# Attention with a bias table and a feed-forward layer: batch 1's v staged in fp32 and cast by GpSimd, q and k transposed by head, the band table loaded pair by pair

## The chip, the cores and the metric

The kernel runs on one core of one Trainium2 chip. The core has TensorE (PE: matrix products and transposes into PSUM), VectorE (DVE), ScalarE (ACT), GpSimd (POOL) and SyncE (SP, which here only issues transfers). Each engine works through its own queue in order and waits on semaphores. Transfers are issued by SP (hardware queue), by ACT (one) and by GpSimd (software queue, which alone converts types on the way); all run on the same 16 DMA engines. The metric is the device time of one execution in microseconds, the median of several runs.

## The reference

```python
B, H, S, D = 8, 8, 576, 64            # q, k, v: fp32, 0.1 * randn
scores = (q @ k.transpose(0, 1, 3, 2)) / sqrt(D)
scores = scores + bias_table[bucket].transpose(2, 0, 1)[None]   # bucket from |i - j|: 32 buckets, constant from 128 on
attn = softmax(scores)
x = (attn @ v).transpose(0, 2, 1, 3).reshape(B * S, H * D)      # 4608 x 512
h = x @ w_in                                                     # 512 x 2048
out = maximum(0.01 * h, h) @ w_out                               # 2048 x 512, fp32
```

## The kernel before, in words

**Attention.** The work is cut into 32 items: 8 batches by 4 pairs of heads. For an item n, `rows` (L385) copies q and k of the pair next to each other, `turn_by_pe` (L395) transposes them on TensorE (later items by DMA, `turn_by_dma`), `take_turned` (L407) copies the result from PSUM to `qt` and `kt`, and `apart` (L411) puts the last 64 positions of both heads apart. `score` (L432 to L440) makes the transposed scores in six units, `expo` (L446 to L453) takes their exponential on ACT, and `band` (L465) multiplies the part near the diagonal by the exponential of the bias difference (far from it the bias is constant and falls out of the softmax). `av` and `av_tail` (L485 to L503) multiply by v, which carries a column of ones for the sum; `norm` (L512, L513) divides. The result is transposed into `xT` (L527 and L531, or by DMA).

**Feed-forward.** The 4608 tokens are cut into nine tiles of 512. `ffn_in` (L544) makes 16 groups of four matmuls per tile, `ffn_act` (L549) applies the leaky relu, `ffn_out` (L556) makes the output, `ffn_y` (L561) copies it and `ffn_store` sends it.

**Buffers.** q, k and v of a batch sit in one of two sets in bf16 (`qn`, `kn`, `vn` with the first 512 positions, `v4` with the last 64). Probabilities have three sets in the first batch (`at_` twice and `spare`, in the tile `extra`), then two. The pool `gt` has two buffers, which hold `first` (raw q, k of pair 0 and raw v of batch 0) and `extra`, and later the activations of the token tiles in turn. PSUM: two tiles for scores, one for AV, three for all else.

**Loads.** Batch 0's v comes as fp32 by SP (`load_v_raw`, L312, L314) and is cast by GpSimd (`cast_v`, L333, L336). All other q, k, v and both weights come by GpSimd's queue with the cast in the transfer (`load_qk` L195, `load_v` L225 and L230, `load_v_part` L203 and L209, `load_w_in` L351, `load_w_out` L357). The table: `shift_table`, `exp_table`, `spread_table`, `copy_u_row` and `store_u_row` write one row per head to DRAM (L308); `load_hk` (L318) and `load_hk4` (L325) read it back as a band, shifted by one per partition.

**Order.** Nothing is ordered by hand past the first few lines. Each piece of work is a task in `Plan` with an engine, a cost in us, the tasks it comes after and a rank. `Plan.order` simulates the five queues with these costs and the PSUM slots, and always takes the task that can start first; the program is issued in this order, and each engine's queue keeps it. GpSimd's transfers are modelled as one ring, by `moves`; what the program's semaphores make GpSimd wait for ahead of an issue is not in the model. `run` adds matmuls on junk data (`spin`) where the plan sees TensorE idle early on. First-layer groups of a token tile have ranks from 10000, so they fill the time that attention leaves.

Of the kernel before, what the change touches and what calls it, by code (L numbers as in the profile page):

```python
# [36 lines left out]
class Plan:  # L37


    LAG = 0.25  # L40

    def __init__(self, slots):
        self.tasks = []
        self.slots = {k: [0.0] * v for k, v in slots.items()}

# [7 lines left out]
    def link(self, ins):  # L53

        for t in self.tasks:
            t["after"] = [ins[d[1:]] if isinstance(d, tuple) else d for d in t["after"]]
            t["behind"] = [d for d in t["after"] if d["engine"] == t["engine"] == "POOL"]
            t["after"] = [d for d in t["after"] if not any(d is o for o in t["behind"])]

    def order(self):  # L60
# [4 lines left out]
        first = False  # L65
        while any(waiting.values()):
# [35 lines left out]
            if t["rank"] >= 10000 and e == "PE" and not first:  # L102
                first = True
                self.slots["M"].append(r)
                t["first"] = True
# [3 lines left out]
    def run(self, fill):  # L109

        fills = True
        for t in self.order():
            if t.get("first"):
                fills = False
            if fills and t["engine"] == "PE" and t["start"] > 6.0:
# [7 lines left out]
def kernel(  # L123
# [90 lines left out]
    def load_v(b, h0, h1, by_head):  # L214
        i = b % NBUF
        p0, p1 = h0 // 2, h1 // 2
        if by_head:
            for h in range(h0, h1):
                nc.gpsimd.dma_start(
                    out=vn[i][:, :, h, 0:D],  # L220
                    in_=v[b, h, 0 : NJ * P, :].rearrange("(c s) d -> s c d", s=P),
                )
        else:
            for c in range(NJ):
                nc.gpsimd.dma_start(  # L225
                    out=vn[i][:, c, h0:h1, 0:D],
                    in_=v[b, h0:h1, c * P : (c + 1) * P, :].rearrange("h s d -> s h d"),
                )
        for e in range(2):
            nc.gpsimd.dma_start(  # L230
                out=v4[i][e * SL : (e + 1) * SL, p0:p1, e, 0:D],
                in_=v[b, h0 + e : h1 : 2, NJ * P : S, :].rearrange("h s d -> s h d"),
            )
# [18 lines left out]
    vraw_sb = first[:, qk_e : qk_e + NJ * H * D].rearrange("p (c h d) -> p c h d", c=NJ, h=H)  # L252
    vraw4 = first[:, qk_e + NJ * H * D : qk_e + (NJ * H + n_pairs) * D].rearrange("p (h d) -> p h d", h=n_pairs)
    extra = gt_pool.tile([P, n_fc, TT], BF16, name="extra", tag="gt").rearrange("p f t -> p (f t)")
    spare = extra[:, 0 : ATW + SL], extra[:, ATW + SL : ATW + SL + S + SL]
# [5 lines left out]
    load_qk(0, 2, 4)  # L261
    load_qk(0, 4, 6)
# [22 lines left out]
    clear_v(nc.gpsimd, 0)  # L285
    for i in range(3):
        clear_edges(nc.gpsimd, i)
    clear_v(nc.gpsimd, 1)
# [21 lines left out]
    def load_v_raw():  # L310
        for c in range(NJ):
            nc.sync.dma_start(out=vraw_sb[:, c, :, :], in_=v[0, :, c * P : (c + 1) * P, :].rearrange("h s d -> s h d"))  # L312
        for e in range(2):
            nc.sync.dma_start(out=vraw4[e * SL : (e + 1) * SL, :, :],  # L314
                                in_=v[0, e::2, NJ * P : S, :].rearrange("h s d -> s h d"))

# [13 lines left out]
    def cast_v(c):  # L330

        if c < NJ:
            nc.gpsimd.tensor_copy(out=vn[0][:, c, :, 0:D], in_=vraw_sb[:, c, :, :])  # L333
            return
        for e in range(2):
            nc.gpsimd.tensor_copy(out=v4[0][e * SL : (e + 1) * SL, :, e, 0:D], in_=vraw4[e * SL : (e + 1) * SL, :, :])  # L336

    def gate(t, row=0):
        nc.gpsimd.tensor_copy(out=w_in_sb[row : row + 1, 0, 0:1], in_=t)

# [11 lines left out]

    def load_w_out(half):
        if half > 1:
            return
        n = n_fc // 2
        nc.gpsimd.dma_start(  # L357
            out=w_out_sb[:, half * n : (half + 1) * n, :],
            in_=moe_w_out[half * n * P : (half + 1) * n * P, :].rearrange("(f p) e -> p f e", p=P),
        )  # L360

# [29 lines left out]

    def turn_by_pe(n, j):
        ps = turned[n, j] = ps_m_pool.tile([P, 8 * P], BF16, name="ps_t", tag="m")
        for c in range(NC):
            nc.tensor.transpose(ps[:, c * RQ : (c + 1) * RQ], in_=prs[n][0:RQ, j, c, :],  # L395
                                identity=ident[0:RQ, 0:RQ])
# [139 lines left out]
    def ffn_in(T, f0):  # L536
        t0, w = tiles[T]
        if f0 == 0:
            gts[T] = gt_pool.tile([P, n_fc, TT], BF16, name="gt", tag="gt")
        pm = pms[T, f0] = ps_m_pool.tile([P, TT], FP32, name="pm1", tag="m")  # L540
        for j in range(TT // w):
            f = f0 + j
            for c in range(n_cc):
                nc.tensor.matmul(pm[:, j * w : (j + 1) * w], lhsT=w_in_sb[:, c, f * P : (f + 1) * P],  # L544
                                 rhs=xT[c][:, t0 : t0 + w], start=(c == 0), stop=(c == n_cc - 1))

    def ffn_act(T, f0):
        t0, w = tiles[T]
        nc.scalar.activation(gts[T][:, f0 : f0 + TT // w, 0:w], pms.pop((T, f0)).rearrange("p (j t) -> p j t", t=w),  # L549
                             AF.Prelu, bias=0.0, scale=1.0, alpha=0.01)  # L550
# [17 lines left out]
    plan = Plan({"S": 2, "O": 1, "M": 2})  # L568
# [7 lines left out]
    L["raw", 0], L["raw", 1], tabl = dma(4.0), dma(4.2), dma(3.8)  # L576
    sh = add("DVE", 0.1, [tabl], shift_table, -1)
    e8t = add("ACT", 0.25, [sh], exp_table, -1)
    spr = add("PE", 0.4, [e8t], spread_table, -1, take=["O"])
    cpu = add("DVE", 0.6, [spr], copy_u_row, -1, give=["O"])  # L580
    urt = add("SP", 0.1, [cpu], store_u_row, -1, tail=2.8)
    hkt = add("SP", 0.1, [urt], lambda: load_hk(0, 2), -1, tail=3.2)
    hkr = add("SP", 0.1, [urt], lambda: (load_hk(2, H), load_hk4()), 1, tail=5.5)
    vrt = add("SP", 0.5, [urt], load_v_raw, 2, tail=6.0)
    vrt["land"] = 18.0
    L["hk", 0], L["hk", 1] = hkt, hkr
# [10 lines left out]
    QK, VB, WH = 3.9, 9.5, 5.6  # L597
    L["qk", 0, 0], L["qk", 0, 1] = dma(7.0), dma(9.5)
    pool_load(("qk", 0, 2), 1.6, lambda: (gate(ub[0:1, 0:1]), load_qk(0, 6, H)), QK / 2, after=[cpu])
    pool_load(("w_in", 0), 1.0, lambda: (gate(vraw4[SL : SL + 1, 0, 0:1], SL), load_w_in(0)), WH, after=[vrt])  # L600
    vc = [add("POOL", 0.6, [vrt] + prev, lambda c=c: cast_v(c), 0) for c in range(NJ + 1)]
    vt[0] = vc[-1]
    pool_load(("qk", 1, 0), 1.6, lambda: load_qk(1, 0, 4), QK)
    vt[1] = pool_load(("v", 1), 5.5, lambda: load_v(1, 0, H, False), VB)
    pool_load(("w_in", 1), 0.8, lambda: load_w_in(1), WH)
    pool_load(("qk", 1, 1), 1.6, lambda: load_qk(1, 4, H), QK)
    pool_load(("w_out", 0), 0.9, lambda: load_w_out(0), WH)
    pool_load(("w_out", 1), 0.9, lambda: load_w_out(1), WH)

    def plan_rows(n):  # L610
# [6 lines left out]
        if n == 0:  # L617
            r0 = add("DVE", 0.6, [L["raw", 0]], lambda: rows(0, 0), feed)
            r1 = add("ACT", 0.75, [L["raw", 1]], lambda: rows(0, 1), feed)
        else:  # L620
# [7 lines left out]
        else:  # L628
            g = [add("PE", 0.28, [(r0, r1)[j]] + sct.get(n - NQT, []) + wait, lambda j=j: turn_by_pe(n, j), feed, take=["M"])
                 for j in range(2)]  # L630
            rowt[n] = [r0, r1] + g
            src, give = g, ["M"]
        on_act = n < n_pairs - 1 or n == n_pairs
        cq = add("ACT" if on_act else "DVE", 0.6 if on_act else 0.75, [src[0]] + sct.get(n - NQT, []),
                 lambda c=nc.scalar.copy if on_act else nc.vector.tensor_copy: take_turned(n, 0, c), feed, give=give)
        on_act = n == n_pairs
        ck = add("ACT" if on_act else "DVE", 0.6 if on_act else 0.75, [src[1]] + sct.get(n - NQT, []),
                 lambda: take_turned(n, 1, nc.scalar.copy if n == n_pairs else nc.vector.tensor_copy), feed, give=give)
        on, cost = ("POOL", 0.5) if n in (1, 2) else ("DVE", 0.2)
        ak = add(on, cost, [ck], lambda: apart(n, kts[n]), feed + 1)  # L640
        aq = add(on, cost, [cq], lambda: apart(n, qts[n]), feed + 1)
# [7 lines left out]
    def plan_pair(n):  # L649
# [27 lines left out]
        sct[n] = ss  # L677
        cost = [0.43, 0.56, 0.56, 0.48, 0.25]
        bt = [add("DVE", cost[c], [es[u] for u in ([c], [c], [c], [3, 4], [5])[c]] + [L["hk", 0 if n == 0 else 1]],
                  lambda c=c: band(n, c), soon + 3) for c in range(NJ + 1)]  # L680
        done = list(es.values()) + bt + [vt[b]]
        tail_of[n] = [es[NJ + 1], bt[NJ], vt[b]]
# [25 lines left out]
    def plan_ffn(T):  # L708
# [3 lines left out]
        for f in range(n_fc):  # L712
            i = ins[T, f] = add("PE", 0.866, need + [L["w_in", int(f >= n_fc // 2)]] + (oin[T - 2] if T > 1 else []),
                                lambda f=f: ffn_in(T, f), 10000 + T * 64 + f * 4, take=["M"])
# [13 lines left out]
    for n in range(N):  # L728
        if n >= 2 * n_pairs and n % n_pairs == 0:
# [45 lines left out]
```

## Time and profile before

| | |
|---|---|
| time, median of 3 runs | 389.34 us (388.59 to 389.54) |
| time of the profiled execution | 389.1 us |
| its span, first to last instruction | 387.3 us |
| busy, us: PE, DVE, ACT, POOL | 372.1, 202.9, 241.7, 68.6 |
| mean granted TensorE clock | 0.986 |
| moved by DMA | 40.62 MB, mean 105 GB/s |

Times in the rows are in us from the start of the span, durations of one instruction in ns where marked. In rows of the order of time stand start, duration, engine, line, operation and operands, then in brackets how long the engine was idle before it and what released it. In rows of the stretches stand, for each engine, the busy time and the number of instructions, then the granted clock, the busy share of the DMA engines and what they moved. PE is a matmul, PEld a weight load. The releaser is inferred; where several semaphores were waited for, it can be the wrong one.

### The profile page before, as it was taken

What the parts mean: (1) busy time and instruction counts of PE and PEld (TensorE: products, weight loads), DVE (VectorE), ACT (ScalarE), POOL (GpSimd) and SP (SyncE); (2) the same over time, 40 slices, a digit from 0 to 9 for tenths busy, and PEclk for the clock granted to TensorE, in tenths of its full rate; (3) what the DMA queues carried; (4) which work ended last, traced back from release to release, by engine and by line L of the source; (5) the groups of instructions that cost most, each with busy time, mean ns of one, the idle gap of its engine ahead of it and who ended that gap; (6) DMA issues with size and microseconds to landing.
All of it is one profiled execution on the core that took longest, in us unless ns stands there. A gap on an engine that the chain in (4) does not pass through costs nothing.

```text
span 387.3 us, 8302 instructions
## 1 busy us (share of the span) xinstructions
PE 372.1 (96%) x3388; PEld 188.8 (49%) x3388; DVE 202.9 (52%) x539; ACT 241.7 (62%) x345; POOL 68.6 (18%) x112
## 2 busy tenths in 40 slices
PE   6859899999999999999999999999999999999995
PEld 2337455555554455555545454545545644444442
DVE  6837637878676756757565756545634411001021
ACT  4946697558975798579758875877587533333300
POOL 7168314017003300510060004000000000000000
PEclk9968999999999999999999999999999999999999
DMA  7969999759996994998399949611121100101012
GB/s 130 229 111 180 207 206 166 141 99 141 180 125 114 167 150 71 105 191 111 70 119 163 115 91 111 72 46 44 47 46 46 47 27 27 56 27 54 29 54 81
DMA packets 102741, 40.62 MB, mean 105 GB/s; under 512 B 81704, under 2 KB 97072, under 8 KB 102704
## 3 DMA queue, kind: packets, MB, share of 16 engines
q0 software_dynamic: 48512, 17.47, 42.0%
q1 hardware_dynamic: 53984, 22.33, 30.7%
q8 instruction: 26, 0.43, 0.5%
q10 hardware_dynamic: 208, 0.29, 0.3%
q14 instruction: 11, 0.09, 0.1%
HBM read 37.69 MB, written 9.45 MB: 122 GB/s over the span
## 4 chain that ended last, share of the span: by engine, by line
PE 88%; DVE 3%; SPq 3%; DMA 2%; ACT 1%; POOL 1%; issue 0%; DVEq 0%; POOLq 0%
PE pm L544 32%; PE pm L556 32%; PE ps_s L432 8%; PE ps_om L500 5%; PE ps_o L500 5%; PE ps_s L436 2%; PE ps_s L439 2%; SPq L312 1%; DMA tab<-in_bias_table_dram 1%; DVE opair L513 1%; DMA first<-in_v_dram 1%; PE ps_o L485 1%; ACT at L446 1%; DVE at L465 1%; POOL vn L333 1%; PE ps_t L395 0%
## 5 line engine op out<-in xcount | busy, mean ns | idle before, releaser
L544 PE MATMUL pm<-xT,w_in_sb 128*128 128x512 bf16 x576 | 140.6, 380 | 1.1 <-ACT gt L549 1.0
L446 ACT ACTIVATE at<-ps_s 128x1024 bf16<-128x1024 f32 x124 | 120.6, 1030 | 33.1 <-PE ps_s L432 32.5
L556 PE MATMUL pm<-w_out_sb,gt 128*128 128x512 bf16 x576 | 138.8, 380 | 0.0
L549 ACT ACTIVATE gt<-pm 128x512 bf16<-128x512 f32 x144 | 84.4, 606 | 62.1 <-PE pm L544 61.1
L465 DVE TENSOR_TENSOR at<-at,hk 128x768 bf16<-128x768 bf16 (+3 forms) x155 | 67.9, 453 | 35.3 <-ACT at L446 27.3
L556 PEld LDWEIGHTS <-gt 128*128 128x128 bf16 x576 | 53.9, 98 | 65.8 <-issue 4.7
L544 PEld LDWEIGHTS <-w_in_sb 128*128 128x128 bf16 x576 | 52.4, 98 | 65.7 <-issue 8.9
L561 DVE COPY y<-pm 128x512 f32<-128x512 f32 x36 | 24.8, 689 | 72.0 <-PE pm L556 72.0
L203 POOL DMA_DIRECT2D vn<-in_v_dram x24 | 21.6, 908 | 147.3 <-PE ps_o L500 141.6
L500 PEld LDWEIGHTS <-at 128*128 128x128 bf16 x1240 | 42.8, 99 | 6.8 <-issue 4.9
L432 PE MATMUL ps_s<-qt,kt 64*128 64x512 bf16 x256 | 40.2, 384 | 1.1 <-ACT at L453 0.3
L500 PE MATMUL ps_o<-vn,at 128*128 128x65 bf16 x640 | 27.0, 196 | 4.1 <-POOL vn L333 4.1
L448 ACT ACTIVATE at<-ps_s 128x512 bf16<-128x512 f32 x31 | 18.5, 598 | 16.7 <-PE ps_s L436 16.7
L512 DVE RECIPROCAL rcp<-ps_om 128x5 f32<-128x5 f32 x31 | 6.0, 195 | 38.6 <-PE ps_om L500 37.6
L500 PE MATMUL ps_om<-vn,at 128*128 128x65 bf16 x600 | 24.6, 196 | 0.0
L407 DVE COPY qt<-tu 128x576 bf16<-128x576 bf16 x22 | 15.6, 710 | 13.1 <-PE ps_s L440 13.1
L432 PEld LDWEIGHTS <-kt 64*128 64x128 bf16 x256 | 8.4, 94 | 27.4 <-issue 25.4
L453 ACT ACTIVATE at<-ps_s 128x576 bf16<-128x576 f32 x31 | 20.2, 652 | 0.0
L513 DVE TENSOR_TENSOR opair<-ps_o,rcp 128x320 bf16<-128x320 f32 x33 | 16.2, 492 | 1.1
L513 DVE TENSOR_TENSOR opair<-ps_om,rcp 128x320 bf16<-128x320 f32 x31 | 15.2, 492 | 1.3 <-DVE rcp L512 0.3
L407 DVE COPY kt<-tu 128x576 bf16<-128x576 bf16 x22 | 15.1, 686 | 0.0
L439 PE MATMUL ps_s<-qt,kt 128*128 128x512 bf16 x32 | 12.4, 387 | 0.9 <-ACT at L446 0.9
(80 smaller groups left out, 234.1 us busy)
## 6 DMA issues: line engine op xcount, KB each, us to landing
out_dram<-y SPq DMA_DIRECT2D x36, 256.0 KB, 2.0
qn<-in_q_dram POOLq DMA_DIRECT2D x14, 288.0 KB, 10.0
kn<-in_k_dram POOLq DMA_DIRECT2D x14, 288.0 KB, 11.7
vn<-in_v_dram POOLq DMA_DIRECT2D x28, 128.0 KB, 6.0
w_in_sb<-in_moe_w_in_dram POOLq DMA_DIRECT2D x2, 1024.0 KB, 9.7
w_out_sb<-in_moe_w_out_dram POOLq DMA_DIRECT2D x2, 1024.0 KB, 17.9
first<-in_v_dram SPq DMA_DIRECT2D x4, 256.0 KB, 6.5
hk<-u_row SPq DMA_DIRECT2D x1, 576.0 KB, 6.2
```

What stands on the lines that cost most here:

```text
L203: nc.gpsimd.dma_start(out=vn[i][:, c, :, 0:D], in_=v[b, :, c * P : (c + 1) * P, :].rearrange("h s d -> s h d"),)
L407: copy(out=t[:, 0:S].rearrange("p (r c) -> p r c", c=NC), in_=src)
L432: nc.tensor.matmul(ps[:, e, :], lhsT=kt[r, u * P : (u + 1) * P], rhs=qt[r, 0:512], start=True, stop=True)
L446: nc.scalar.activation(at[:, :, u, 0:512], ps, AF.Exp, scale=scale)
L453: nc.scalar.activation(at4[:, 0:S], ps.rearrange("p e i -> p (e i)")[:, 0:S], AF.Exp, scale=scale)
L465: nc.vector.tensor_tensor(out=o, in0=o, in1=m, op=ALU.mult)
L500: nc.tensor.matmul(ps[:, ic, :], lhsT=at[:, o : o + P], rhs=vn[i][:, c, 2 * p + e, :], start=whole and c == 0, stop=not whole and ic == NJ ...
L513: nc.vector.tensor_tensor(out=opairs[n][:, :, e * D : (e + 1) * D], in0=ps[:, :, 0:D], in1=rcp.to_broadcast([P, NJ + 1, D]), op=ALU.mult)
L544: nc.tensor.matmul(pm[:, j * w : (j + 1) * w], lhsT=w_in_sb[:, c, f * P : (f + 1) * P], rhs=xT[c][:, t0 : t0 + w], start=(c == 0), stop=(c ...
L549: nc.scalar.activation(gts[T][:, f0 : f0 + TT // w, 0:w], pms.pop((T, f0)).rearrange("p (j t) -> p j t", t=w), AF.Prelu, bias=0.0, scale=1 ...
L556: nc.tensor.matmul(ys[T, ts], lhsT=gts[T][:, f, ts * P : (ts + 1) * P], rhs=w_out_sb[:, f, :], start=(f == 0), stop=(f == n_fc - 1))
L561: nc.vector.tensor_copy(out=y, in_=ys[T, ts])
```

## The change

Batch 0's v is loaded by GpSimd's queue, not SP's, still in fp32 into `first`: heads 0 and 1 first, the other six behind (`stage_v`); `cast_v` casts them in two steps. Batch 1's v, which came with the cast in the transfer, is now staged in fp32 too, in a new tile `staged` of the pool `gt`, and cast by GpSimd. In the plan its cast has rank 35, while both halves of w_out have rank 21; its load, the second part of batch 1's q and k, and w_out are planned after pair 2's AV. Pairs 1 to 4 are transposed by head, straight from `qn` and `kn`, with 24 transposes for 12 and without `rows`. The band table is loaded with one transfer per pair. Batch 0's buffers are cleared ahead of the first loads, the others later. The one-row copies by which loads were held back (`gate`) are gone. The first two first-layer groups are split, three chunks ahead and the fourth behind. The plan has three PSUM slots for all else from its time 26 on (before: from the first first-layer group on), and some costs and ranks differ.

In GpSimd's queue as built, batch 1's cast stands behind the loads of batch 2's q, k and v:

```
... staged<-v x6 | memsets | qn,kn (batch 1, heads 4 to 7) | w_out x2 | qn,kn,qn,kn (batch 2) | vn x4, v4 x2 (batch 2) | cast vn (batch 1), v4 x2 | qn,kn (batch 3) ...
```

```diff
-    def load_v(b, h0, h1, by_head):
...
+    def stage_v(b, h0, h1):
+        m, t = stage_views(b)
+        if h1 - h0 < NJ:
             for h in range(h0, h1):
+                nc.gpsimd.dma_start(out=m[:, :, h, :], in_=v[b, h, 0 : NJ * P, :].rearrange("(c s) d -> s c d", s=P))
         else:
             for c in range(NJ):
+                nc.gpsimd.dma_start(out=m[:, c, h0:h1, :],
+                                    in_=v[b, h0:h1, c * P : (c + 1) * P, :].rearrange("h s d -> s h d"))
         for e in range(2):
+            nc.gpsimd.dma_start(out=t[e * SL : (e + 1) * SL, h0 // 2 : h1 // 2, :],
+                                in_=v[b, h0 + e : h1 : 2, NJ * P : S, :].rearrange("h s d -> s h d"))
+
+    def cast_v(b, h0, h1):
+        m, t = stage_views(b)
+        nc.gpsimd.tensor_copy(out=vn[b][:, :, h0:h1, 0:D], in_=m[:, :, h0:h1, :])
+        for e in range(2):
+            r = slice(e * SL, (e + 1) * SL)
+            nc.gpsimd.tensor_copy(out=v4[b][r, h0 // 2 : h1 // 2, e, 0:D], in_=t[r, h0 // 2 : h1 // 2, :])
...
+    def by_heads(n):
+        return 0 < n <= n_pairs
+
     def turn_by_pe(n, j):
...
+                b, p = items[n]
+                for e in range(2):
+                    nc.tensor.transpose(ps[e * D : (e + 1) * D, c * RQ : (c + 1) * RQ],
+                                        in_=(qn, kn)[j][b % NBUF][0:RQ, 2 * p + e, c, :], identity=ident[0:RQ, 0:RQ])
...
-    hkr = add("SP", 0.1, [urt], lambda: (load_hk(2, H), load_hk4()), 1, tail=5.5)
-    vrt = add("SP", 0.5, [urt], load_v_raw, 2, tail=6.0)
...
+    hk4t = add("SP", 0.1, [urt], load_hk4, 0, tail=5.0)
+    for p in range(n_pairs):
+        L["hk", p] = hkt if p == 0 else add("SP", 0.1, [urt], lambda p=p: load_hk(2 * p, 2 * p + 2), p, tail=4.2 + 2.0 * p)
...
-    pool_load(("qk", 0, 2), 1.6, lambda: (gate(ub[0:1, 0:1]), load_qk(0, 6, H)), QK / 2, after=[cpu])
-    pool_load(("w_in", 0), 1.0, lambda: (gate(vraw4[SL : SL + 1, 0, 0:1], SL), load_w_in(0)), WH, after=[vrt])
-    vc = [add("POOL", 0.6, [vrt] + prev, lambda c=c: cast_v(c), 0) for c in range(NJ + 1)]
-    vt[0] = vc[-1]
-    pool_load(("qk", 1, 0), 1.6, lambda: load_qk(1, 0, 4), QK)
-    vt[1] = pool_load(("v", 1), 5.5, lambda: load_v(1, 0, H, False), VB)
-    pool_load(("w_in", 1), 0.8, lambda: load_w_in(1), WH)
-    pool_load(("qk", 1, 1), 1.6, lambda: load_qk(1, 4, H), QK)
-    pool_load(("w_out", 0), 0.9, lambda: load_w_out(0), WH)
-    pool_load(("w_out", 1), 0.9, lambda: load_w_out(1), WH)
+    pool_load(("qk", 0, 0), 1.4, lambda: load_qk(0, 2, 4), QK / 2, after=[dma(2.4)], rank=-9)
+    pool_load(("qk", 0, 1), 1.4, lambda: load_qk(0, 4, 6), QK / 2, rank=-9)
+    pool_load(("v", 0, 0), 2.8, lambda: stage_v(0, 0, 2), VS / 4 + 1.0, rank=-9)
+    edges = add("POOL", 1.0, list(prev), lambda: [clear_edges(nc.gpsimd, i) for i in range(3)], -8)
+    pool_load(("qk", 0, 2), 1.4, lambda: load_qk(0, 6, H), QK / 2 + 1.0, rank=-8)
+    pool_load(("v", 0, 1), 4.5, lambda: stage_v(0, 2, H), 3 * VS / 4 + 1.0, rank=-5)
+    pool_load(("qk", 1, 0), 1.4, lambda: load_qk(1, 0, 4), QK, rank=-4)
+    pool_load(("w_in", 0), 0.8, lambda: load_w_in(0), WH, after=[hkr], rank=-4)
+    vt[0] = [add("POOL", 1.2, [L["v", 0, 0]], lambda: cast_v(0, 0, 2), 5),
+             add("POOL", 2.4, [L["v", 0, 1]], lambda: cast_v(0, 2, H), 5)]
+    add("POOL", 1.2, list(prev), lambda: clear_v(nc.gpsimd, 1), 9)
+    pool_load(("w_in", 1), 0.8, lambda: load_w_in(1), WH, rank=6)
+
+    def late_loads():
+        pool_load(("v", 1, 0), 5.0, lambda: (new_stage(), stage_v(1, 0, H)), VS, after=avt[2], rank=20)
+        pool_load(("qk", 1, 1), 1.4, lambda: load_qk(1, 4, H), QK, rank=20)
+        pool_load(("w_out", 0), 0.9, lambda: load_w_out(0), WO, rank=21)
+        pool_load(("w_out", 1), 0.9, lambda: load_w_out(1), WO, rank=21)
+        vt[1] = add("POOL", 3.2, [L["v", 1, 0]], lambda: cast_v(1, 0, H), 35)
...
+                early = [add("PE", 0.65, [t for p in range(n_cc - 1) for t in nmt[p]] + w + xt[n_cc - 1][:f],
+                             lambda f=f: ffn_in(T, f, range(n_cc - 1)), rank - 3, take=["M"])]
```

More of the change, by code (lines that the diff above doesn't have):

```diff
@@ L56, in link @@
             t["after"] = [ins[d[1:]] if isinstance(d, tuple) else d for d in t["after"]]
-            t["behind"] = [d for d in t["after"] if d["engine"] == t["engine"] == "POOL"]
+            t["behind"] = [d for d in t["after"] if d["engine"] == "POOL" and "moves" in t]
             t["after"] = [d for d in t["after"] if not any(d is o for o in t["behind"])]
@@ L109, in run @@
     def run(self, fill):
[L111 removed]
         for t in self.order():
[L113 to L115 removed]
+            if t["engine"] == "PE" and 6.0 < t["start"] < self.WARM:
                 k = int((t["idle"] - 0.3) / 0.25)
@@ L534, with ffn_in, ffn_act @@
     tiles = [(T * TT, TT) for T in range(n_tt)]
-    def ffn_in(T, f0):
+    def ffn_in(T, f, cs=range(n_cc)):
         t0, w = tiles[T]
[L538 to L550, printed above, removed]
+        if cs[0] == 0:
+            if f == 0:
+                gts[T] = gt_pool.tile([P, n_fc, TT], BF16, name="gt", tag="gt")
+            pms[T, f] = ps_m_pool.tile([P, TT], FP32, name="pm1", tag="m")
+        for c in cs:
+            nc.tensor.matmul(pms[T, f], lhsT=w_in_sb[:, c, f * P : (f + 1) * P], rhs=xT[c][:, t0 : t0 + w],
+                             start=(c == 0), stop=(c == n_cc - 1))
+    def ffn_act(T, f):
+        nc.scalar.activation(gts[T][:, f, :], pms.pop((T, f)), AF.Prelu, bias=0.0, scale=1.0, alpha=0.01)
     def ffn_out(T, ts, i):
```

125 lines of the change are left out of this document (51 added, 74 removed).

## The prediction

> **What bounds the kernel now.** I read the page first, then busy time by stretches, then the waits, then GpSimd's and TensorE's instructions in order of time. From the page:
>
> ```profile
> span 387.3 us, 8302 instructions
> ```
>
> The stretches (time, then busy us and instruction count of PE, PEld, DVE, ACT, POOL, then granted TensorE clock, DMA share, GB/s):
>
> ```profile
> 5.00:10.00 5.00, 3.29 (x34) 1.68 (x34) 3.50 (x9) 2.89 (x5) 3.29 (x15) 1.00 0.85 114
> 15.00:20.00 5.00, 3.84 (x21) 1.47 (x19) 4.12 (x12) 5.00 (x7) 0.00 (x0) 1.00 1.28 214
> 20.80:24.00 3.20, 0.10 (x3) 0.10 (x2) 0.67 (x2) 1.48 (x2) 1.66 (x4) 0.63 0.01 3
> 24.00:26.00 2.00, 0.85 (x5) 0.41 (x4) 0.00 (x0) 0.00 (x0) 1.95 (x4) 0.50 0.92 115
> 26.00:31.80 5.80, 5.80 (x81) 4.67 (x80) 2.91 (x8) 1.76 (x3) 5.79 (x9) 0.50 1.17 205
> 56.10:60.00 3.90, 3.78 (x80) 3.04 (x77) 2.75 (x7) 3.00 (x5) 1.51 (x2) 1.00 1.32 205
> 60.00:380.00 320.00, 319.95 (x2854) 160.22 (x2852) 165.39 (x430) 201.04 (x289) 38.57 (x51) 1.00 0.67 92
> ```
>
> From 60 us on TensorE has no gap (319.95 of 320.00), so only two things can change the end: when TensorE reaches that full stretch with how much work left, and any new hole in it. The visible hole is at 20.8 to 26, where TensorE, ACT and DMA all stand, with a half clock until 31.8. The waits say why:
>
> ```profile
> ACT extra L446 <- PE ps_s L432: 5.6, 1, 5.6
> ...
> POOL vn L203 <- DMA w_out_sb<-in_moe_w_out_dram: 4.1, 1, 4.1
> PE ps_o L500 <- POOL vn L333: 4.1, 4, 3.1
> ...
> ACT extra L453 <- PE ps_s L440: 1.3, 1, 1.3
> ```
>
> TensorE's first attention-times-v (AV) waits for GpSimd's cast of batch 0's v (L333), and ACT then waits for scores queued behind it: 5.6 + 1.3 = 6.9 us that can be had back. The other row matters more to me: GpSimd is held by a transfer. Its issue of vn waits until w_out has landed. GpSimd's queue:
>
> ```profile
> 4.13 0.57 POOL L236 MEMSET v<- 128x520 bf16 x1
> 4.75 0.26 POOL L238 MEMSET v<- 64x4 bf16 x2
> 5.07 0.24 POOL L239 MEMSET vn<- 128x32 bf16 x1
> ...
> 23.34 2.28 POOL L333 CAST vn<-first 128x512 bf16<-128x512 f32 x4
> 25.55 0.86 POOL L336 CAST v<-first 64x256 bf16<-64x256 f32 x2
> ...
> 52.22 0.87 POOL L203 DMA_DIRECT2D vn<-in_v_dram  x1 [4.14 <-DMA w_out_sb<-in_moe_w_out_dram]
> 57.86 0.88 POOL L203 DMA_DIRECT2D vn<-in_v_dram  x1 [4.76 <-PE ps_o L500]
> 58.82 0.63 POOL L209 DMA_DIRECT2D v<-in_v_dram  x1
> 60.27 0.62 POOL L209 DMA_DIRECT2D v<-in_v_dram  x1 [0.82 <-PE ps_tx L527]
> ```
>
> In the program as built, GpSimd's transfers take eight completion semaphores in turn, and each issue first waits until the transfer eight places earlier has landed. The waits of 4.14 and 4.76 us, the steps to 52.22 and from there to 57.86, are the two halves of w_out landing (the second row names a TensorE matmul, but the program has it wait for the second half of w_out and for pair 3's AV, long done). These issues load batch 2's v; nothing needs it soon, so before the change the hold is free.
>
> **The new wait.** In the changed kernel's GpSimd queue the order is: staged load of batch 1's v, rest of batch 1's q and k, both halves of w_out, batch 2's four q/k loads, batch 2's six v loads, and only then the cast of batch 1's v from its staging buffer. The fifth and sixth of batch 2's v loads wait for batch 2's first q and k loads, which sit behind both halves of w_out in the transfer queue. So the cast cannot start until everything that ends at 60.27 + 0.62 = 60.9 us before the change has been moved. TensorE's queue puts pair 4's AV, which needs that cast, behind 13 first-layer groups and ahead of all that follows; nothing passes it. Before the change that AV starts at 56.10:
>
> ```profile
> 41.09 1.03 PE L544 MATMUL pm<-xT,w_in_sb 128*128 128x512 bf16 x4
> ...
> 46.67 2.76 PE L544 MATMUL pm<-xT,w_in_sb 128*128 128x512 bf16 x12
> ...
> 56.10 0.19 PE L485 MATMUL ps_o<-v,at 64*128 64x65 bf16 x1
> ...
> 57.59 0.67 PE L395 MATMUL ps_t<-ident,pr 96*128 96x96 bf16 x12
> 58.10 1.03 PE L544 MATMUL pm<-xT,w_in_sb 128*128 128x512 bf16 x4
> ```
>
> **The sum, at that AV.** First, how much earlier the transfers run. The hole is filled, since batch 1's q and k and w_in are now issued before v's cast and not behind it: 3.2 x (1 - 3/205) + 2.0 x (1 - 115/205) = 3.15 + 0.88 = 4.0 us earlier. A second hole, 5 to 10 us, is 5 x (1 - 114/205) = 2.2 us wide; filling it could give that, but the clearing of batch 0's v buffers now stands ahead of the first issue (0.57 + 0.26 + 0.24 = 1.1 us), and small issues then follow each other at their own pace. I bound it by -1.1 and +1.1 net. Batch 1's v now arrives as fp32, twice the bytes; sizes of one load, and GpSimd's issues that waited for the first vn and the first v4 load of batch 1 before:
>
> ```profile
> vn<-in_v_dram POOLq DMA_DIRECT2D x28, 128.0 KB, 6.0
> ...
> first<-in_v_dram SPq DMA_DIRECT2D x4, 256.0 KB, 6.5
> ...
> 34.70 0.67 POOL L195 DMA_DIRECT2D kn<-in_k_dram  x1 [0.30 <-DMA vn<-in_v_dram]
> ...
> 39.39 0.67 POOL L195 DMA_DIRECT2D kn<-in_k_dram  x1 [0.58 <-DMA v<-in_v_dram]
> ```
>
> Between those two lie three loads of 128 KB and one of 32 KB, 416 KB in 4.7 us; all of it (576 KB) is then 6.5 us. Staged, 1152 KB (1.18 MB) at 205 GB/s is 5.8 us. So the rate is no worse for it; I take no difference, bounds -0.7 and +0.7. Together: 4.0 us earlier, bounds 2.2 and 5.8. Then the cast: 2.28 + 0.86 = 3.1 us by batch 0's rows (same tiles). Pair 4's AV starts at 60.9 - 4.0 + 3.1 = 60.0, bounds 58.2 and 61.8: **3.9 us later** than 56.1.
>
> Work moved ahead of it: TensorE has then done one more group of four (2.76 us for three groups, so 0.9) and pair 6's twelve transposes (57.59 to 58.10, 0.51) than before at that point: **1.4 us back**.
>
> The clock: TensorE gets there at about 56.1 - 6.9 + 1.4 = 50.6 and stands 9 us. Standing from 20.8 to 24 was enough to halve the clock, and from 26.0, with TensorE filled, the half clock lasted 5.8 us more, which costs 2.9 us of work. The same here: **2.9 us**, bounds 1.5 and 4.4 (half and one and a half of the one instance). The Trainium skill (TensorE: Matmul & The Clock Gate, "What's actually happening") says that the clock is judged in free-running windows of about 3.4 us and returns after one busy window. This trace's stretch at half clock (3.2 x 0.37 / 0.5 + 2.0 + 5.8 = 10.2 us) is three such windows long; by the page the stretch after the stall would be 3.4 to 6.8 us, an estimate of 1.7 to 3.4 us lost, and the sum would be 0.5 above or 1.2 below mine.
>
> Sum: 3.9 - 1.4 + 2.9 = +5.4 us. The profiled execution took 389.1 us for a span of 387.3, a quarter of a us under the median 389.34; 389.1 + 5.4 = **394.5 us**.
>
> **What is costed at nothing, and by what cover.** All the gains ahead of that AV fall into its 9 us of standing: v of batch 0 in hand earlier (up to 6.9), the row copies dropped for pairs 1 to 4, the first two groups started with three of four chunks. So do the costs: 24 transposes for 12 in four pairs (4 x 0.51 = 2.0 us of TensorE), q and k of batch 0 about 1 us later, the table row stored after pair 0's transposes, and band tables that come pair by pair beside a busy transfer queue. Any of these could be several us late without showing at the end. If the cover goes, they count in full. Past that AV the queues hold the same work; the second token tile's buffer is the staging buffer and waits for the same cast, which is done by then.
>
> GpSimd's casts of batch 0's v now run while DVE is busy (before, DVE did nothing at 24 to 26). If they slowed, w_in's two halves, issued around them, keep the transfer queue full for some 9 us: w_out's two halves, of the same size, hold GpSimd for 4.14 and 4.76 us in the rows above. The Trainium skill (SBUF — State Buffer, "SBUF: two separate sides") says that GpSimd and a DVE copy in a two-port mode exclude each other, and that this can starve transfers whose descriptors GpSimd writes. No row here shows a cast of GpSimd slowed by DVE.
>
> **Rivals.**
> 1. The cast is not late: the transfer queue runs much faster than 205 GB/s once fed without a break, or the semaphore waits do not hold it. Then pair 4's AV starts when TensorE arrives and the 6.9 us are gained, less 0.5 for pair 4's extra transposes: 389.1 - 6.4 = 382.7. It decides when the cast ends before 50.6, 9 us ahead of my sum. For it: the hole at 20.8 is really removed. Against: 205 GB/s at 26 to 31.8 and again at 56.1 to 60, with the queue full, looks like a ceiling, and the rows 52.22 and 57.86 show GpSimd held. 0.08.
> 2. The cast ends at 56 to 57 and the clock falls for a short time only: gains and costs cancel, 389. 0.05.
> 3. GpSimd is slowed by DVE at 17 to 25 us (no row shows it; the page just named states such a rule): casts and issues of batch 0 there take twice as long (3.1 us of casts and about as much of issues), the queue runs dry for some 3 us ahead of batch 1's v, and everything behind is as much later: 397.5. For it: DVE is busy 4.12 of 5 us at 15 to 20. Against: w_in's 9 us of cover. 0.09.
>
> That the change does not do what it says I leave out: the order of the queues is fixed in the built program.
>
> **The numbers.** My forecast has 0.78, at 394.5, with its own bounds: +2.1 - 1.4 + 1.5 = 2.2 (391.3) and +5.7 - 1.4 + 4.4 = 8.7 (397.8). To hold 8 in 10 I reach down towards rival 2 and take 390.7 to 398.3; rival 1 lies outside. A measurement here tells about 0.3%, 1.2 us, from no change. Faster 0.08 (rival 1), same 0.05 (rival 2), slower 0.87.
>
> **What would show it.** TensorE idle for some 9 us just before the first AV on batch 1's v, released by GpSimd's cast; that cast directly behind batch 2's v loads, which wait on w_out; its end at about 60 us; granted clock 0.5 for 4 to 7 us of full work behind it; ACT without the 5.6 us wait at 22 to 28; first-layer groups starting near 34 us instead of 41.09; no gap in the transfers at 20 to 26. I am wrong if the AV does not wait (rival 1), if the clock stays full, or if holes appear after 70 us.

## The result, and the profile after

| | before | after |
|---|---|---|
| time, median | 389.30 us (388.59 to 389.54, 4 runs) | 394.67 us (394.07 to 395.49, 4 runs) |
| ratio to before, 95% interval | | 1.0142 [1.0118, 1.0167] |
| profiled execution: time, span | 389.1, 387.3 us | 395.03, 393.1 us |
| mean granted TensorE clock | 0.986 | 0.978 |

The changed kernel is slower by 1.4%. A second measurement gave 394.53 us (393.76 to 395.02, 4 runs), ratio 1.0131 [1.0114, 1.0149].

GpSimd's queue of the changed kernel in order of time (start, duration, engine, line, operation; in brackets the idle time before and its releaser):

```profile
36.34 0.89 POOL L331 DMA_DIRECT2D w_out_sb<-in_moe_w_out_dram  x1 [0.53 <-DMA staged<-in_v_dram]
37.66 0.88 POOL L331 DMA_DIRECT2D w_out_sb<-in_moe_w_out_dram  x1 [0.42 <-DMA staged<-in_v_dram]
...
49.66 1.08 POOL L196 DMA_DIRECT2D vn<-in_v_dram  x1 [3.51 <-PE pm L525]
55.45 0.87 POOL L196 DMA_DIRECT2D vn<-in_v_dram  x1 [4.70 <-DMA w_out_sb<-in_moe_w_out_dram]
...
57.94 0.61 POOL L202 DMA_DIRECT2D v<-in_v_dram  x1 [0.99 <-DMA kn<-in_k_dram]
58.60 1.89 POOL L228 CAST vn<-staged 128x2048 bf16<-128x2048 f32 x1
60.43 0.85 POOL L231 CAST v<-staged 64x256 bf16<-64x256 f32 x2
```

These rows answer to 52.22, 57.86 and 60.27 of before. GpSimd stands 3.51 and 4.70 us while the halves of w_out land. The releaser named in the first of the two is a TensorE matmul, as in before's second one; in the program this issue also waits for the transfer eight places ahead of it, which is w_out's first half, and in the second profile of this kernel the same row (at 50.27, after 4.48 us) names w_out. The cast of batch 1's v (L228, L231) has no wait of its own. The chain of waits that ended last shows how long its data had been there (start, duration):

```profile
26.14 15.12 DMA staged<-in_v_dram
41.83 15.58 DMA kn<-in_k_dram
58.60 1.89 POOL vn L228
```

The staged v has landed by 26.14 + 15.12 = 41.3 us; its cast begins 17.3 us later, behind an issue that waited for batch 2's k, which landed at 41.83 + 15.58 = 57.4. TensorE's queue:

```profile
37.99 0.82 PE L525 MATMUL pm<-xT,w_in_sb 128*128 128x512 bf16 x3
...
52.99 0.60 PE L414 MATMUL ps_s<-qt,kt 64*128 64x512 bf16 x4
60.88 0.21 PE L467 MATMUL ps_o<-v,at 64*128 64x65 bf16 x1 [7.29 <-POOL v L231]
```

The first row answers to 41.09 of before (first-layer work starts 3.1 us earlier), the third to 56.10: pair 4's AV starts 4.8 us later, after 7.29 us of standing. The stretches (busy us and count of PE, PEld, DVE, ACT, POOL; granted clock; DMA share; GB/s):

```profile
20.00:26.00 6.00, 2.50 (x56) 1.79 (x51) 5.93 (x15) 3.25 (x5) 5.60 (x8) 0.93 1.22 209
49.00:59.00 10.00, 4.42 (x31) 2.04 (x30) 3.02 (x8) 5.49 (x9) 3.60 (x5) 0.84 1.68 190
59.00:64.00 5.00, 2.87 (x51) 2.66 (x51) 0.69 (x2) 0.00 (x0) 4.83 (x7) 0.50 2.02 87
64.00:70.00 6.00, 6.00 (x44) 2.83 (x42) 3.21 (x9) 3.68 (x7) 0.00 (x0) 0.82 1.18 179
100.00:380.00 280.00, 280.00 (x2456) 139.18 (x2453) 137.06 (x353) 179.17 (x260) 28.76 (x38) 1.00 0.58 87
```

The hole in the transfers at 20 to 26 us is gone (209 GB/s where before had 3 at 20.8 to 24). The clock is half for 3.2 of the 10 us from 49 to 59, for all of 59 to 64, and at 0.82 from 64 to 70, that is until about 66.2. Of this the 5.3 us from 60.88 on hold work, which costs 2.6 us. From 100 us on TensorE has no gap.

TensorE and ACT still have a hole at the old place, though. Rows of DVE (the division after pair 0's AV), TensorE (pair 1's AV) and ACT:

```profile
25.57 0.49 DVE L495 TENSOR_TENSOR opair<-ps_o,rcp 128x320 bf16<-128x320 f32 x1
26.12 0.40 PE L482 MATMUL ps_o<-vn,at 128*128 128x65 bf16 x4 [3.56 <-DVE opair L495]
28.79 1.94 ACT L428 ACTIVATE at<-ps_s 128x1024 bf16<-128x1024 f32 x2 [5.53 <-PE ps_s L414]
```

Now v is there, but TensorE waits for DVE, which is busy for 5.93 of the 6 us from 20 to 26 and comes to this division only behind its band multiplications. The clock falls here too: from 26 to 32 us it is half in this profile, and 0.83 and 0.60 (26 to 29, 29 to 32) in the second one, so a profile's mean clock (0.978 and 0.987) does not price the stall alone. TensorE is ready for pair 4's AV at 53.6 in the one and at 53.5 in the other, so at the end neither shows.

A balance from the AV's start to the end of the span needs nothing else: before 387.3 - 56.10 = 331.2 us, after 393.1 - 60.88 = 332.2, and 331.2 - 1.4 (work moved ahead) + 2.6 (clock) = 332.4. So +4.8 at the AV, -1.4 and +2.6 give +6.0, and the span grew by 5.8.

### The profile page after: what moved, and what is told of

Its sections match the earlier page's. It is cut to its first block, busy times and chain, and to the rows that moved or that the text cites. A ratio compares the mean times of both kernels' runs of the same rounds, so it can differ in the third digit from the quotient of the medians.

```text
span 393.1 us, 8378 instructions
## 1 busy us (share of the span) xinstructions
PE 372.7 (95%) x3427; PEld 189.5 (48%) x3427; DVE 199.7 (51%) x528; ACT 243.2 (62%) x348; POOL 79.7 (20%) x123
## 4 chain that ended last, share of the span: by engine, by line
PE 83%; DMA 8%; POOL 7%; issue 1%; DVE 1%; POOLq 0%
PE pm L535 32%; PE pm L525 29%; PE ps_s L414 7%; PE ps_om L482 5%; PE ps_o L482 4%; DMA kn<-in_k_dram 4%; DMA staged<-in_v_dram 4%; PE ps_s L418 1%; PE ps_s L421 1%; POOL vn L228 1%; PE ps_o L467 1%; POOL first L220 1%; POOL staged L220 1%; POOL kn L188 1%; POOL v L231 1%
## 5 line engine op out<-in xcount | busy, mean ns | idle before, releaser
L529 ACT ACTIVATE gt<-pm 128x512 bf16<-128x512 f32 x144 | 84.3, 607 | 72.3 <-PE pm L525 71.6
L447 DVE TENSOR_TENSOR at<-at,hk 128x768 bf16<-128x768 bf16 (+3 forms) x155 | 68.8, 458 | 39.7 <-ACT at L428 26.3
L494 DVE RECIPROCAL rcp<-ps_om 128x5 f32<-128x5 f32 x31 | 6.0, 194 | 44.4 <-PE ps_om L482 44.0
L482 PE MATMUL ps_om<-vn,at 128*128 128x65 bf16 x600 | 25.1, 198 | 0.0
L389 DVE COPY qt<-tu 128x576 bf16<-128x576 bf16 x22 | 15.5, 704 | 15.9 <-PE ps_s L422 11.9
L467 PE MATMUL ps_o<-v,at 64*128 64x65 bf16 x135 | 8.7, 191 | 7.3 <-POOL v L231 7.3
```

The costliest lines, as they stand in the source:

```text
L389: copy(out=t[:, 0:S].rearrange("p (r c) -> p r c", c=NC), in_=src)
L447: nc.vector.tensor_tensor(out=o, in0=o, in1=m, op=ALU.mult)
L482: nc.tensor.matmul(ps[:, ic, :], lhsT=at[:, o : o + P], rhs=vn[i][:, c, 2 * p + e, :], start=whole and c == 0, stop=not whole and ic == NJ ...
L529: nc.scalar.activation(gts[T][:, f, :], pms.pop((T, f)), AF.Prelu, bias=0.0, scale=1.0, alpha=0.01)
```

## The experiments

Each is the changed kernel with one edit, except where another base is named. "Rest" is the time from the start of pair 4's AV to the end of the span.

| kernel | median us | ratio to before on the same chip | AV at | span | rest |
|---|---|---|---|---|---|
| cast first | 384.60 | 0.9877 [0.9855, 0.9900] | 51.76 | 381.3 | 329.5 |
| the same again | 383.38 | 0.9843 [0.9824, 0.9863] | 50.70 | 380.3 | 329.6 |
| w_out behind the cast | 387.53 | 0.9957 [0.9940, 0.9973] | 52.18 | 385.4 | 333.2 |
| before, with a late cast | 400.94 | 1.0302 [1.0286, 1.0318] | 65.21 | 399.2 | 334.0 |
| junk in the stall | 394.29 | 1.0133 [1.0091, 1.0174] | 61.83 | 391.9 | 330.1 |
| junk in the stall, again | 393.58 | 1.0095 [1.0069, 1.0120] | 61.76 | 391.8 | 330.0 |
| the changed kernel again | 394.53 | 1.0131 [1.0114, 1.0149] | 61.33 | 393.0 | 331.7 |
| cast first, row copies | 383.72 | 0.9856 [0.9840, 0.9872] | 50.38 | 381.4 | 331.0 |
| the same again | 385.08 | 0.9904 [0.9879, 0.9929] | 50.71 | 381.7 | 331.0 |
| cast first, table in one | 385.33 | 0.9901 [0.9883, 0.9920] | 54.07 | 383.8 | 329.7 |
| cast first, v held back | 383.97 | 0.9858 [0.9833, 0.9884] | 51.99 | 381.6 | 329.6 |

**Is it the cast's place in GpSimd's queue?** The cast is put directly behind w_out's two issues; all other queues keep their order.

```diff
-        pool_load(("w_out", 1), 0.9, lambda: load_w_out(1), WO, rank=21)
-        vt[1] = add("POOL", 3.2, [L["v", 1, 0]], lambda: cast_v(1, 0, H), 35)
+        pool_load(("w_out", 1), 0.9, lambda: (load_w_out(1), cast_v(1, 0, H)), WO, rank=21)
+        vt[1] = add("POOL", 3.2, [L["v", 1, 0]], lambda: None, 35)
```

> The changed kernel with one move in GpSimd's queue: the cast of batch 1's v stands directly behind the two issues of w_out, ahead of batch 2's ten loads; every other engine's queue is as in the changed kernel. Theory (the cast is late only by its place in the queue, behind issues that wait for w_out to land): the cast can start when the staged v has landed, near 42 us, and TensorE, which reached pair 4's AV at 53.5, no longer stands; the 7.3 us of standing and the 2.6 us lost at half clock go: 394.7 - 9.9 = 384.8 us. Rival A (the transfers themselves are the bound, w_out and batch 2 are needed just behind): a new hole of several us appears between 55 and 80 us and the time stays above 390. Rival B (the transposes by head and the band table pair by pair cost the time, the standing only hides it): the time stays above 389.

384.60 us, as expected; GpSimd's and TensorE's rows of this kernel:

```profile
41.55 1.89 POOL L228 CAST vn<-staged 128x2048 bf16<-128x2048 f32 x1 [2.40 <-DMA staged<-in_v_dram]
...
51.76 0.19 PE L467 MATMUL ps_o<-v,at 64*128 64x65 bf16 x1
```

Now the cast waits only for its data, and the AV has no wait: it starts when TensorE arrives. The rest is 329.5, close to 331.2 less 1.4, with the clock full. So the whole loss, and the gain that it hid, hang on this one place. The second measurement:

> The kernel with the cast directly behind w_out's issues once more, unaltered, on one chip with the next two. 384.6 us as before.

383.38 us. This version beats both kernels, by 1.2 to 1.6% of before. The two medians lie 1.2 us apart, and that is how closely kernels measured at different times can be compared.

**Is it w_out's landing, or the ten issues themselves?** The cast stays behind batch 2's loads, but w_out is issued behind the cast.

```diff
-        pool_load(("w_out", 0), 0.9, lambda: load_w_out(0), WO, rank=21)
-        pool_load(("w_out", 1), 0.9, lambda: load_w_out(1), WO, rank=21)
-        vt[1] = add("POOL", 3.2, [L["v", 1, 0]], lambda: cast_v(1, 0, H), 35)
+        pool_load(("w_out", 0), 0.9, lambda: None, WO, rank=21)
+        pool_load(("w_out", 1), 0.9, lambda: None, WO, rank=21)
+        vt[1] = add("POOL", 3.2, [L["v", 1, 0]], lambda: (cast_v(1, 0, H), load_w_out(0), load_w_out(1)), 35)
```

> The changed kernel with w_out's two loads issued behind the cast of batch 1's v; the cast stays behind batch 2's ten loads, all other queues as in the changed kernel. Theory (it is w_out's landing that holds those loads and with them the cast): the cast ends near 51 us, before TensorE comes at 53.5, no standing at pair 4's AV; w_out lands about 10 us later than before, so the first output groups may wait 1 to 4 us: 386 to 389 us. Rival (any ten loads ahead of the cast hold it as long, w_out or not): TensorE still stands some 7 us at pair 4's AV and the time stays near 394.7 or above.

```profile
47.20 1.89 POOL L228 CAST vn<-staged 128x2048 bf16<-128x2048 f32 x1
...
52.18 0.19 PE L467 MATMUL ps_o<-v,at 64*128 64x65 bf16 x1
```

Behind the same ten loads the cast now starts at 47.20 and not 58.60, and the AV does not wait. The ten issues alone are not the hold; the landing of w_out, which they had to wait for, is. What this order gives away stands in its waits from 50 us on (engine, tile and line, releaser: us in total, times, longest):

```profile
PE pm L535 <- DMA w_out_sb<-in_moe_w_out_dram: 3.4, 2, 2.1
```

TensorE's first output groups wait 3.4 us for w_out, and the rest is 333.2, 3.7 over that of the kernel before this.

**The late cast alone.** The kernel before the change gets only the staging of batch 1's v in fp32 and its cast behind batch 2's loads; TensorE, DVE and ACT keep their queues.

```diff
-    vt[1] = pool_load(("v", 1), 5.5, lambda: load_v(1, 0, H, False), VB)
+    pool_load(("v", 1), 5.5, lambda: stage_v(), VB)
+    vt[1] = add("POOL", 3.2, [L["v", 1]], cast_staged, 35)
...
+            vt[1]["after"].append(vt[2])
```

> The kernel before with this part of the change alone: batch 1's v staged in fp32 and cast by GpSimd behind batch 2's loads; the queues of TensorE, DVE and ACT are those of the kernel before. Theory: the cast starts when the last of batch 2's issues is out, 60.9 us, ends at 63.6, TensorE stands 7.5 us at pair 4's AV and then loses about 2.6 us at half clock: 389.3 + 10.1 = 399.4 us. Rival (the late cast matters only together with the rest of the change, or staging by itself is cheap): within 2 us of 389.3.

```profile
62.27 0.61 POOL L209 DMA_DIRECT2D v<-in_v_dram  x1 [0.82 <-DMA kn<-in_k_dram]
62.93 1.89 POOL L249 CAST vn<-staged 128x2048 bf16<-128x2048 f32 x1
64.76 0.86 POOL L252 CAST v<-staged 64x256 bf16<-64x256 f32 x2
...
65.21 0.21 PE L504 MATMUL ps_o<-v,at 64*128 64x65 bf16 x1 [8.75 <-POOL v L252]
```

400.94 us, 1.5 more than forecast. The AV starts 65.21 - 56.10 = 9.1 us later and the rest grows by 2.8, together the 11.9 us of the span. It also prices a term that I had at nothing. The last of batch 2's loads ends at 62.27 + 0.61 = 62.88, where before had 60.89, 2.0 us later. Not all of this is the staging: the issue that ends the hole in the transfers, w_in's first half, was late already, ahead of the first staged transfer. Its row before, then here:

```profile
22.47 0.81 POOL L351 DMA_DIRECT2D w_in_sb<-in_moe_w_in_dram  x1 [0.30 <-POOL w_in_sb L339]
```

```profile
23.30 0.81 POOL L370 DMA_DIRECT2D w_in_sb<-in_moe_w_in_dram  x1 [0.30 <-POOL w_in_sb L358]
```

That is 0.8 us that the edit does not explain, and leaves 1.2 us for fp32 staging. It is one profile of each, and the last load of the changed kernel moved by 0.4 us between its two profiles (57.94 and 58.39), so this holds to about half a us.

**The clock.** 32 matmuls on junk data ahead of pair 4's AV keep TensorE busy in the stall.

```diff
+        if n == n_pairs:
+            ps_w_pool[0] = ps_m_pool.tile([P, 512], FP32, name="ps_w", tag="m")
+            spin(32)
```

> The changed kernel with 32 matmuls on junk data put into TensorE's queue just ahead of pair 4's AV, 6.9 us of work at full clock that fits into the 7.3 us of standing. Theory (the half clock behind the standing is a cost of its own): the standing stays until near 61 us, the clock stays full behind it, and 2.6 us are gained: 392.1 us. Rival (the half clock is hidden behind other waits, or the late cast alone makes up all of the loss): 394.7 within 0.5.

394.29 us (392.23 to 396.21, 4 runs) is near the rival's 394.7, but its runs spread over both theories' times; so it ran again, beside the changed kernel on one chip.

> The changed kernel with 32 junk matmuls on TensorE ahead of pair 4's AV, which fill the stall and keep the clock up; once more, since the first time lay between the two theories. That the stall's clock costs 2.6 us: the clock stays full, the part from pair 4's AV to the end is 2 us shorter than in the changed kernel, and the time is about 2.1 to 2.6 us under the changed kernel's on the same chip, 392.1 to 392.6 if that is 394.7, unless the junk ends behind the cast. That the half clock costs nothing at the end: no difference, 394.7.

> The changed kernel once more, unaltered, so that the kernel with 32 junk matmuls in the stall is compared with it on one chip. Time as measured first, 394.7 us; in the profile TensorE's clock at half for about 10 us from the middle of the stall on, of which about 5 us lie behind the start of pair 4's AV, and 332 us from that start to the end of the span.

The junk and the stretches of that second run, then the stretches of the changed kernel beside it:

```profile
53.64 7.08 PE L746 MATMUL ps_w<-junk 128*128 128x512 bf16 x32
...
61.76 0.19 PE L470 MATMUL ps_o<-v,at 64*128 64x65 bf16 x1 [1.04 <-POOL v L231]
...
59.00:64.00 5.00, 3.68 (x60) 2.37 (x59) 0.67 (x3) 0.00 (x0) 4.89 (x7) 1.00 2.33 105
64.00:70.00 6.00, 6.00 (x48) 3.02 (x47) 3.56 (x11) 4.96 (x8) 0.78 (x2) 1.00 1.26 176
```

```profile
61.33 0.21 PE L467 MATMUL ps_o<-v,at 64*128 64x65 bf16 x1 [7.87 <-POOL v L231]
...
59.00:64.00 5.00, 2.42 (x44) 2.21 (x44) 0.49 (x2) 0.00 (x0) 4.79 (x8) 0.50 2.35 77
64.00:70.00 6.00, 6.00 (x52) 3.13 (x50) 3.41 (x10) 3.73 (x7) 0.46 (x1) 0.87 1.28 186
```

With the junk the clock is full, and the rest is 330.0 and 330.1 us; without it 332.2 and 331.7. By the clock column the changed kernel lost 2.6 us in its first profile and (65.6 - 61.33) / 2 = 2.1 in its second; the rest differs by 2.1 to 2.2 and by 1.6 to 1.7. So the half clock does reach the end. By the medians it is less: 394.53 to 393.58, and the intervals of the two ratios overlap a little. In the two profiles with junk the cast ended some 0.4 to 1.0 us later than in the two without, which takes part of the gain back. The junk in the stall, from 53.6 us on, is not the cause: GpSimd's issue of batch 1's other q, which waits for w_in, is late already, at 31.1 against 30.1 and 30.4. What made it late is open.

**The by-head transposes without their cover.** To the kernel with the cast first, pairs 1 to 4 get their row copies and 12 transposes back.

```diff
     def by_heads(n):
-        return 0 < n <= n_pairs
+        return False
```

> The kernel with the cast directly behind w_out's issues (384.6 us), and in it pairs 1 to 4 transposed in the old way, from row copies, 12 transposes a pair. There the stall that covered TensorE's extra transposes is gone. If each transpose counts at its price and nothing stands in their place: pair 1 to 4's 48 transposes saved are 48 x 0.043 = 2.0 us, so 382.6. If TensorE ahead of pair 4's AV waits for other things anyway (the band table, scores), or the row copies that come back on DVE cost as much: 384.6. If the row copies, on DVE's queue ahead of the band multiplications, delay the scores: 385.5 to 387.

> The kernel with the cast first and row copies for pairs 1 to 4, once more, on one chip with the one that has the transposes by head. If the 0.9 us between their medians is real: 383.7 against 384.6. If not, no difference beyond 0.3%.

Inconclusive in time: 383.72 us, then 385.08 where the kernel with transposes by head had 383.38 on the same chip. The saving of 2.0 us is not seen in either, and the second pair even points the other way. The spans (381.4 and 381.7 against 381.3 and 380.3) say why the AV's start misleads here: it comes at 50.38 and 50.71, but the plan put 44 first-layer matmuls ahead of it and not 52, two groups of 0.92 us, and the rest is 1.4 to 1.5 us longer.

**The table pair by pair.** To the kernel with the cast first, one transfer for heads 2 to 7.

```diff
-        L["hk", p] = hkt if p == 0 else add("SP", 0.1, [urt], lambda p=p: load_hk(2 * p, 2 * p + 2), p, tail=4.2 + 2.0 * p)
+        if p < 2:
+            L["hk", p] = hkt if p == 0 else add("SP", 0.1, [urt], lambda: load_hk(2, H), 1, tail=6.2)
+        else:
+            L["hk", p] = L["hk", 1]
```

> The kernel with the cast directly behind w_out's issues (384.6 us), and in it the band table of heads 2 to 7 again loaded with one transfer instead of three. If the table pair by pair is worth something: pair 1's band multiplication comes later by the longer transfer, 1 to 3 us, of which TensorE, no longer covered by the stall, loses all or part: 385.6 to 387.6. If pair 1 waits for other things as long: 384.6.

385.33 us: by the medians 0.7 us over the first measurement of its base and 1.9 over the second, in the spans 2.5 and 3.5. The AV starts 2.3 and 3.4 us later, with the same rest. Its transfers (size, median us from issue to landing), then those of the base:

```profile
hk<-u_row SPq DMA_DIRECT2D x1, 576.0 KB, 11.3
```

```profile
hk<-u_row SPq DMA_DIRECT2D x4, 192.0 KB, 8.4
```

With the one large transfer DVE has to wait for pair 1's band, which the base does not:

```profile
24.26 1.93 DVE L447 TENSOR_TENSOR at<-at,hk 128x512 bf16<-128x512 bf16 x5 [0.93 <-DMA hk<-u_row]
```

So the table by pairs seems to be worth something once nothing covers the place. The medians say 0.7 to 1.9 us, but two measurements of the base lie 1.2 us apart, so the size is open. In the changed kernel 7.3 us of standing lay over it.

**Why the first band was late.** SP's issues and DVE's first band multiplication, before the change and after:

```profile
7.36 0.32 SPq L308 DMA_DIRECT2D u_row<-ub  x1
8.65 0.92 SPq L318 DMA_DIRECT2D hk<-u_row  x2
...
13.75 1.75 DVE L465 TENSOR_TENSOR at<-at,hk 128x512 bf16<-128x512 bf16 x4
```

```profile
8.16 0.32 SPq L301 DMA_DIRECT2D u_row<-ub  x1
11.03 0.42 SPq L304 DMA_DIRECT2D hk<-u_row  x1
...
17.46 2.65 DVE L447 TENSOR_TENSOR at<-at,hk 128x512 bf16<-128x512 bf16 x5 [6.01 <-DMA hk<-u_row]
```

The store of one row per head took 2.9 us where it took 1.3, and the band came 3.7 us later. I took the bulk of v (heads 2 to 7, issued from 9.1 us on) to be the cause of both, and held it back in the kernel with the cast first.

```diff
-    pool_load(("v", 0, 1), 4.5, lambda: stage_v(0, 2, H), 3 * VS / 4 + 1.0, rank=-5)
+    pool_load(("v", 0, 1), 4.5, lambda: ([clear_edges(nc.gpsimd, i) for _ in range(4) for i in range(3)], stage_v(0, 2, H)), 3 * VS / 4 + 1.0, rank=-5)
```

> The kernel with the cast first, and in it GpSimd clears the probabilities' edges four times over ahead of its issues of v's heads 2 to 7 (24 small memsets, some 2.1 us), so that these transfers, of 576 KB, start 2 us later; all other queues are as they were. If it is the bulk of v that slows the table's store (2.5 us from SP's issue at 8.17 to the first load of the band) and the band's load behind it: the load of the band is issued 1 us earlier, DVE's wait of 6.7 us for it falls by 1.5 us or more, pair 4's AV comes about 1 us earlier and the time is 383.6 to 384.6. If it is not: the wait stays at 6.7 us, v comes 2 us later, which batch 0's cast and all transfers behind it share, and the time is 384.6 to 386.6.

```profile
8.20 0.33 SPq L301 DMA_DIRECT2D u_row<-ub  x1
10.62 0.42 SPq L304 DMA_DIRECT2D hk<-u_row  x1
...
14.36 1.76 DVE L447 TENSOR_TENSOR at<-at,hk 128x512 bf16<-128x512 bf16 x4 [2.86 <-DMA hk<-u_row]
```

The same rows of its base:

```profile
8.17 0.33 SPq L301 DMA_DIRECT2D u_row<-ub  x1
10.67 0.42 SPq L304 DMA_DIRECT2D hk<-u_row  x1
...
18.13 1.91 DVE L447 TENSOR_TENSOR at<-at,hk 128x512 bf16<-128x512 bf16 x4 [6.67 <-DMA hk<-u_row]
```

Half right. The band's load is slowed by the bulk of v: issued at the same time, it let DVE start at 14.36, 3.8 us earlier than in this profile of the base (18.13). The size is rough: in the five profiles of kernels with the same queues up to there whose row names the band's load, this one among them, DVE started between 16.3 and 20.1. The store is not slowed by it: it took 2.4 us with the bulk held back and 10.67 - 8.17 = 2.5 in the base. What slows the store is open; batch 0's other q and k and the first part of v are the transfers that stand ahead of it. And the earlier band is worth nothing here: 383.97 us beside 383.38 on the same chip, with overlapping intervals. DVE then waits for the next parts of the band (1.77 us at 17.89, 0.39 at 20.87) and comes to pair 0's first division at 25.1, against 25.9 and 24.9 in the two profiles of the base. Whether v, 2 us later, takes anything away is not separated.

## Why the prediction was right, point by point

- **The new wait.** Right, and shown by three runs: moving the cast alone takes the whole loss away, moving w_out alone takes the stall away, and staging alone brings it into the kernel before. The AV started at 60.88, predicted 60.0 with bounds 58.2 and 61.8.
- **Transfers 4.0 us earlier.** Mis-sized. The last of batch 2's loads ended at 57.94 + 0.61 = 58.55 and not 60.89: 2.3 us earlier, just inside the lower bound of 2.2. The part that is known to have failed is that fp32 staging makes no difference, with bounds of 0.7 either way: the kernel before with staging alone shows about 1.2 us. 4.0 - 1.2 is 2.8; the other half us is not assigned to any step, and is as much as one profile differs from another. The rate was inferred from two waits in GpSimd's queue, which also held the queue's own pace.
- **The cast, 3.1 us.** 58.60 to 61.28 is 2.7 us. One instruction over 2048 columns took 1.89 us where four over 512 had 2.28, and the AV started at 60.88, 0.4 us ahead of the cast's end, as its first head needs only the first of the two short casts. By chance this took back part of the miss before: together +0.9 us.
- **TensorE arrives at 50.6 and stands 9 us.** It arrived at 52.99 + 0.60 = 53.6 and stood 7.3. The gain of 6.9 us at the old hole, from which the 50.6 came, was not had: ACT's wait there, which the prediction expected to go, is 5.53 us and was 5.62. TensorE stands 3.56 us there, no longer for v but for DVE, which started its band multiplications at 17.46 instead of 13.75. First-layer work began at 37.99 where I had put 34. That the stall covers such delays was the step that counted, and it held: the rest of the span shows none of them. Without the stall they do count, a little: the kernel with the cast first arrives at 51.76 and 50.70.
- **Work moved ahead, 1.4 us.** Right: the rest is 329.5 and 329.6 in the kernel with the cast first, and 330.0 and 330.1 with junk in the stall, against 331.2 before.
- **The half clock, 2.9 us.** 2.6 in the first profile, 2.1 in the second. My own term came from a single instance. After pair 4's AV the half clock lasted 5.3, 4.3 and, in the kernel before with the late cast, some 6.4 us; the rows of that one:

```profile
60.00:65.00 5.00, 0.00 (x0) 0.00 (x0) 0.00 (x0) 0.00 (x0) 4.13 (x5) 0.63 1.81 181
65.00:75.00 10.00, 9.53 (x101) 6.52 (x101) 6.02 (x15) 3.64 (x6) 3.17 (x6) 0.67 1.40 145
```

  (65 + 10 x 0.33 / 0.5 = 71.6, less 65.21.) The Trainium skill (TensorE: Matmul & The Clock Gate, "What's actually happening") gives free-running windows of some 3.4 us and the full clock after one busy window. All three durations lie between one and two such windows, so by that rule the term would have been better put as 1.7 to 3.4 us than as 2.9 with ends at 1.5 and 4.4.
- **The sum, 394.5 us.** The mechanism was right, but that the median (394.67) lies so close is luck: the AV came 0.9 us later than in the sum and the half clock cost 0.3 less, and the profiled execution (395.03) lies 0.4 above the median.
- **Rival 1, 382.7 us.** It did not happen, but the kernel that puts the cast first, where its condition is met (the cast ends at 44.4, before 50.6), comes close: its profiled executions took 383.2 and 382.1 us, its medians are 384.60 and 383.38. As a price of the old hole this is luck: ACT still waits there, 5.2 us in all in the first profile and 3.4 in the second. Part of what makes up for it is TensorE's idle time from 35 to 49 us, 1.76 us before and 0.01 there; the other parts no run separates. The argument against this rival took 205 GB/s for a ceiling, which it is not: the changed kernel moved 270 GB/s from 32 to 35 us.
- **Rival 3, GpSimd slowed by DVE.** The first cast of batch 0's v, over 512 columns, took 0.94 us beside a busy DVE, against 0.57 for one of four before. In the second profile of the kernel with the cast first it took 0.64, in eight other profiles 0.61 to 0.67, and in one (cast first, row copies, the second) 0.94 again:

```profile
18.12 0.94 POOL L228 CAST vn<-first 128x512 bf16<-128x512 f32 x1
```

```profile
17.79 0.64 POOL L228 CAST vn<-first 128x512 bf16<-128x512 f32 x1
```

  If there is such an effect, it is some tenths of a us. It could not show at the end: GpSimd waits 4.40 us for w_in to land behind it, at 30.7 to 35.1.

## What to carry to other kernels

Read a queue in program order and ask of every instruction what the ones ahead of it wait for. In these kernels GpSimd, which issues the transfers, waits for old transfers to land, so a piece of work put on it behind ten issues inherits the landing of the large loads in front of them, even where its own data came 17 us ago. A plan that models the transfers but not these waits can put it there. When a hole in one place is closed, price the new wait first and the covered gains and losses second: here one line in one queue turned a loss of 5 us into a gain of 5.

## What the runs showed of the hardware

- A transfer of fp32 into SBUF was not free against one with the cast in the transfer: 1152 KB in place of 576 KB took about 1.2 us longer (62.88 against 60.89, less 0.8 that was there before), in one profile of each.
- Large transfers beside a band load of 192 KB made it land later: DVE, which waits for it, started at 14.36 in the one profile with them held back, and at 16.3 to 20.1 in the five others with the same queues up to there whose row names that load.
- A store of 8 KB took 1.3 us in the kernel before and 2.4 to 2.9 us in the changed one and those made from it; no run here says why.
